# Sums of query-key products over head rows: from TensorE and PSUM to accumulating DMAs, with a new order of the GLU and down blocks

## The chip, the cores and the metric

The kernel runs on one core of one Trainium2 chip. The metric is the device time of one execution in microseconds (us). The core's engines are named as in the profile: PE (TensorE, matrix products into PSUM), DVE (VectorE, elementwise), ACT (ScalarE, here mostly copies out of PSUM), POOL (GpSimd) and SP (SyncE, here the queue that issues nearly all DMAs). Each engine runs its own instructions in order, and engines wait for one another only through semaphores. "SPq" is work of SP's queue; "PEld" is the loading of weights into TensorE, which overlaps its matmuls.

## The reference, cut to what matters

```python
x = A_x                                   # [1, 2048, 640]
xn = layernorm(x)
# A: attention with 32 heads of 20; each position looks at 8 positions, 2 apart, at and before it
qkv = xn @ wqkv                           # wqkv [640, 1920]
logits = sum_d(q * k_gathered) * 20**-0.5 # masked where the position would be below 0
attn = softmax(logits over the 8)
a = sum_w(attn * v_gathered) @ wo         # wo [640, 640]
# B: gated linear unit without a nonlinearity
b = ((xn @ w_gate) * (xn @ w_up)) @ w_down   # 640 -> 1536 -> 640
out = x + a + b
```

Everything is bf16 at the inputs and the output.

## The kernel before, in words

The feature dimension lies on the 128 partitions in five chunks of 128 (`NCH = 5`); time lies along the free dimension. The columns of `wqkv` are taken with stride five (`wcols`, L413), so that one head's 20 features fall on four neighbouring partitions in each of the five chunks: head 0 on partitions 0 to 3, head 31 on 124 to 127. A logit is then a sum over five chunks and four partitions.

**Stages.** First come the layer norm and the transposes to `XNT` (until about 32 us). Then PE runs one long list of work, the "fill": the rest of the Q and K projections (`proj`, L420, 20 items of five matmuls at L424), the V projections (20 items), and then blocks of the GLU and of the output. A GLU block `add_gu(j)` (L719) covers 512 positions with 24 items (12 gate, 12 up, five matmuls each, L577 in `glu`); ACT copies gate into `HT` and up into the ring `USX`, and DVE multiplies them ("h", L582). An output block `add_dn(j)` (L724) covers the same 512 positions with four tiles of 128 rows, each in two halves of 320 columns (`tail`, L592): 12 matmuls with `WD` over `HT` and 5 with `WO` over the attention output in `VO` (L608). DVE then adds the residual `XR` to PSUM and writes `FOUT` ("fin", L612), and SP stores it.

**Attention on DVE.** The sequence is cut in two halves h of 1024 positions. For each half there are four pairs p of window offsets (`pair`, L778; `qk_steps`, L458): DVE multiplies Q with shifted K for three chunks into `SL` (6144 elements a partition) and for two chunks into `TMP` (4096), and adds two of the chunks (L475, 4096), so that three are left. PE then sums the three chunks and the four partitions of each head in one step: `qk_logits` (L478) multiplies with the 0/1 matrix `G`, 12 matmuls a pair, into PSUM banks 6 and 7, which the rest of the fill therefore does not use; ACT scales them into `LOG` (L492), and POOL masks the first positions (L496). `softmax_steps` (L499) is split into a head (three max steps and a subtraction on DVE, the exponential on ACT) and a rest (sums, reciprocal, product). `attn_move` (L530) spreads the result over the head's four partitions in 16 DMAs a half. `pv_steps` (L536) forms the weighted sum of V for 256 positions; there are eight (pv 0 to 7), pv 0 to 3 with the first half's weights. Tile t of the output needs pv number t // 2.

**Order.** One Python program emits all engines' instructions. It keeps two clocks of its own, `t_pe` and `t_dve`, with a booked cost for each step; after each DVE step (`step`, L771) `run_fill` (L747) emits fill items until PE's clock has caught up. This fixes the order on each engine: which copy comes before which exponential on ACT, which h comes before which attention step on DVE. It fixes no times; on the chip an engine waits only for its data and for buffers to come free. The class `Sched` works out the semaphores from the bytes that each instruction reads and writes. Before, the fill's blocks are in the order gu 0, gu 1, dn 0, gu 2, dn 1, gu 3, dn 2, dn 3. `WD` and `WO` share their memory with `SL`, and their loads (`down_loads`, `out_loads`) are put on SP's queue after the last logits.

Of the kernel before, what the change touches and what calls it, by code (L numbers as in the profile page):

```python
# [26 lines left out]
NEG = -1e9  # L27
# [185 lines left out]
def build_kernel(nc, A_x, A_wqkv, A_wo, B_x, B_w_gate, B_w_up, B_w_down, out):  # L213
# [50 lines left out]
    NXR = 3  # L264
    XR = sb("XR", [128, NXR, D])
    FOUT = sb("FOUT", [128, 2, D])
    NUS = 6
# [9 lines left out]
    G = sb("G", [128, H], FP16)  # L277
# [4 lines left out]
    def dma(o, i, r=(), w=(), name="", eng="sp", group=None):  # L282
# [43 lines left out]
    def late_loads():  # L326
        wqkv_load(2)
# [92 lines left out]
    def proj(which, m, j):  # L420
# [9 lines left out]
        op("act", lambda e: e.activation(o, PS[:, b, :], ACT.Copy), r=[PS[:, b, :]], w=[o], name=f"pev{which}_{m}_{j}")  # L430
# [16 lines left out]
    def part_evac(which, t0, nt, m0, nm, b, col):  # L447
# [3 lines left out]
        op("act", lambda e: e.activation(o, i, ACT.Copy), r=[PS[:, b, :]], w=[o], name=f"ppev{which}_{m0}_{t0}")  # L451
# [326 lines left out]
    def pair(h, p):  # L778
# [3 lines left out]
        for it in qk_steps(h, p, s):  # L782
            step(it)
# [84 lines left out]
```

## Time and profile before

| what | value |
|---|---|
| time, median of 3 runs | 262.41 us (262.13 to 262.52) |
| the profiled execution's own time | 262.42 us |
| its span, first to last instruction | 260.7 us |
| TensorE clock granted | 1.000 |
| busy: PE, DVE, ACT, POOL | 255.6, 216.1, 107.3, 6.7 us |
| DMA, mean over the span | 23.46 MB, 90 GB/s |

The profile has several views. The page gives each engine's busy time and, in 40 equal slices of the span (6.5 us each), its busy share in tenths. The chain of waits goes back from the last instruction, at each step to whatever released it. The groups by line give the busy time, the count and the mean duration of one instruction. The timeline gives single instructions with start and duration. A duration holds some overlap with the next instruction of the same engine, so the spacing of two starts in an unbroken run is a better price for one more instruction than its duration.

### The profile page before, as it was taken

Reading aid. Unit: us, or ns where it says so; the run is one execution under the profiler, and the core shown is the slowest. Engines: PE = TensorE matmul, PEld = TensorE weight load, DVE = VectorE, ACT = ScalarE, POOL = GpSimd, SP = SyncE. Lnnn points to the kernel's source line nnn. Section 1 sums busy time; section 2 is a strip of 40 time slices with the busy share of each in tenths; the row PEclk is TensorE's granted clock in tenths of the full one; section 3 lists DMA queues with packets and bytes.
Section 4 is the critical chain, followed back from the end, with each engine's and each line's share of the span. In section 5 each row is a group of like instructions: output and inputs, shape, how many; then the busy total and the mean of one; then the engine's idle time right before and its main releaser. Section 6 shows DMA issues by size and latency. Waiting matters only on the chain.

```text
span 260.7 us, 4018 instructions
## 1 busy us (share of the span) xinstructions
PE 255.6 (98%) x1669; PEld 150.7 (58%) x1669; DVE 216.1 (83%) x240; ACT 107.3 (41%) x193; POOL 6.7 (3%) x13
## 2 busy tenths in 40 slices
PE   7999999899999999999999999999999999999996
PEld 3899855354554444444467744446774444777775
DVE  5799889999999999998847999999999999422221
ACT  3565558555657555565630035551004555000000
POOL 2000050000200000000000000000000000000000
DMA  6968889400000275065001376000311000021301
GB/s 202 326 136 148 100 226 402 156 3 0 0 3 0 50 206 144 0 208 219 3 0 57 97 199 175 0 4 0 99 54 50 0 3 0 27 74 53 101 28 50
DMA packets 21922, 23.46 MB, mean 90 GB/s; under 512 B 9872, under 2 KB 19472, under 8 KB 21904
## 3 DMA queue, kind: packets, MB, share of 16 engines
q1 hardware_dynamic: 21760, 23.04, 31.2%
q8 instruction: 13, 0.21, 0.3%
q10 hardware_dynamic: 144, 0.16, 0.2%
q14 instruction: 5, 0.04, 0.0%
HBM read 14.42 MB, written 2.62 MB: 65 GB/s over the span
## 4 chain that ended last, share of the span: by engine, by line
PE 80%; DVE 14%; SPq 2%; DMA 2%; ACT 1%; issue 1%
PE PS L577 40%; PE PS L608 28%; PE PS L424 10%; DVE SL L467 3%; SPq L283 2%; DVE XNS L371 2%; PE PS L485 2%; DVE STATS L354 2%; DVE SL L475 2%; DVE TMP L467 2%; DVE STATS L348 2%; DMA XST<-in_A_x_dram 2%; DVE MV L360 1%; DVE SD L369 1%; ACT KH L451 0%
## 5 line engine op out<-in xcount | busy, mean ns | idle before, releaser
L577 PE MATMUL PS<-XNT,WG 128*128 128x512 bf16 x240 | 59.6, 379 | 0.0
L577 PE MATMUL PS<-XNT,WU 128*128 128x512 bf16 x240 | 59.6, 379 | 0.0
L608 PE MATMUL PS<-WD,HT 128*128 128x320 bf16 (+1 forms) x396 | 57.6, 295 | 0.0
L579 ACT ACTIVATE HT<-PS 128x512 bf16<-128x512 f32 x48 | 28.7, 598 | 58.2 <-PE PS L577 58.2
L608 PEld LDWEIGHTS PS<-WD,HT 128*128 128x128 bf16 x396 | 38.1, 98 | 14.7
L551 DVE TENSOR_TENSOR PVB<-VO,ATB 128x10240 f16<-128x10240 bf16 x8 | 43.9, 5488 | 0.1
L424 PE MATMUL PS<-XNT,WQKV 128*128 128x512 bf16 x200 | 43.9, 379 | 0.0
L612 DVE TENSOR_TENSOR FOUT<-PS,XR 128x320 bf16<-128x320 f32 (+1 forms) x33 | 15.5, 477 | 30.4 <-PE PS L608 30.1
L577 PEld LDWEIGHTS PS<-XNT,WU 128*128 128x128 bf16 x240 | 23.4, 98 | 28.5 <-issue 0.4
L577 PEld LDWEIGHTS PS<-XNT,WG 128*128 128x128 bf16 x240 | 23.4, 98 | 28.2 <-issue 0.4
L579 ACT ACTIVATE USX<-PS 128x512 bf16<-128x512 f32 x48 | 28.7, 597 | 22.2 <-PE PS L577 20.8
L424 PEld LDWEIGHTS PS<-XNT,WQKV 128*128 128x128 bf16 x200 | 23.3, 118 | 20.2 <-issue 0.8
L546 DVE TENSOR_TENSOR PVB<-PVB 128x5120 f16<-128x5120 f16 (+1 forms) x16 | 34.4, 2150 | 0.0
L467 DVE TENSOR_TENSOR SL<-QH,KH 128x6144 f16<-128x6144 bf16 x8 | 26.8, 3352 | 1.4 <-ACT KH L451 1.4
L608 PE MATMUL PS<-WO,VO 128*128 128x320 bf16 (+1 forms) x165 | 27.1, 295 | 0.0
L582 DVE TENSOR_TENSOR HT<-HT,USX 128x512 bf16<-128x512 bf16 x48 | 18.5, 417 | 4.2 <-ACT USX L579 4.2
L608 PEld LDWEIGHTS PS<-WO,VO 128*128 128x128 bf16 x165 | 15.9, 98 | 5.9
L475 DVE TENSOR_TENSOR SL<-SL,TMP 128x4096 f16<-128x4096 f16 x8 | 18.3, 2290 | 0.2
L467 DVE TENSOR_TENSOR TMP<-QH,KH 128x4096 f16<-128x4096 bf16 x8 | 18.4, 2302 | 0.0
L430 ACT ACTIVATE VO<-PS 128x512 bf16<-128x512 f32 x20 | 11.9, 597 | 9.8 <-PE PS L424 9.8
L437 PE MATMUL PS<-XNT,WQKV 128*128 128x128 bf16 x200 | 12.6, 220 | 0.2
L437 PEld LDWEIGHTS PS<-XNT,WQKV 128*128 128x128 bf16 x200 | 11.6, 118 | 1.2 <-DVE XNT L394 0.5
(49 smaller groups left out, 137.8 us busy)
## 6 DMA issues: line engine op xcount, KB each, us to landing
ATB<-LOG SPq DMA_DIRECT2D x32, 128.0 KB, 2.6
XR<-in_A_x_dram SPq DMA_DIRECT2D x16, 160.0 KB, 2.3
XST<-in_A_x_dram SPq DMA_DIRECT2D x15, 160.0 KB, 3.9
out_dram<-FOUT SPq DMA_DIRECT2D x15, 160.0 KB, 1.8
WG<-in_B_w_gate_dram SPq DMA_DIRECT2D x1, 1920.0 KB, 9.5
WU<-in_B_w_up_dram SPq DMA_DIRECT2D x1, 1920.0 KB, 13.8
WD<-in_B_w_down_dram SPq DMA_DIRECT2D x1, 1920.0 KB, 8.2
WQKV<-in_A_wqkv_dram SPq DMA_DIRECT2D x10, 160.0 KB, 3.8
```

The lines of the kernel that those rows point to most:

```text
L424: op("pe", (lambda l, x, c: lambda e: e.matmul(PS[:, b, :], l, x, start=(c == 0), stop=(c == NCH - 1)))(l, x, c), r=[l, x], w=[PS[:, b, :] ...
L430: op("act", lambda e: e.activation(o, PS[:, b, :], ACT.Copy), r=[PS[:, b, :]], w=[o], name=f"pev{which}_{m}_{j}")
L437: op("pe", (lambda o, l, x, st, sp: lambda e: e.matmul(o, l, x, start=st, stop=sp))(o, l, x, st, sp), r=[l, x], w=[o], name=f"pp{which}_{m ...
L467: return lambda: op("dve", lambda e: e.tensor_tensor(o[:], qw, kw, ALU.mult), r=[q, k], w=[o[:]], name=f"prod{h}_{p}_{c0}")
L475: lambda: op("dve", lambda e: e.tensor_tensor(a, a, b, ALU.add), r=[a, b], w=[a], name=f"psum{h}_{p}")),
L546: return lambda: op("dve", lambda e: e.tensor_tensor(o, x, y, ALU.add), r=[x, y], w=[o], name=f"{name}_{b}")
L551: lambda: op("dve", lambda e: e.tensor_tensor(PVB[:], vw, aw, ALU.mult), r=[v, a], w=[PVB[:]], name=f"pv_{b}")),
L577: op("pe", (lambda l, x, c: lambda e: e.matmul(PS[:, b, :], l, x, start=(c == 0), stop=(c == NCH - 1)))(l, x, c), r=[l, x], w=[PS[:, b, :] ...
L579: op("act", lambda e: e.activation(o, PS[:, b, :], ACT.Copy), r=[PS[:, b, :]], w=[o], name=f"guev{which}_{m}_{j}")
L582: h_pending.append(lambda: op("dve", lambda e: e.tensor_tensor(h, h, o, ALU.mult), r=[h, o], w=[h], name=f"h{m}_{j}"))
L608: op("pe", (lambda l, x, i, b: lambda e: e.matmul(PS[:, b, 0:wid], l, x, start=(i == 0), stop=(i == n - 1)))(l, x, i, b), r=[l, x], w=[PS[ ...
L612: op("dve", (lambda o, xr, b: lambda e: e.tensor_tensor(o, PS[:, b, 0:wid], xr, ALU.add))(o, xr, b), r=[PS[:, b, :], xr], w=[o], name=f"fi ...
```

## The change

- **Logits.** The `G` matmuls, the ACT copies of their results and POOL's mask step go. For each pair, DVE forms the five chunk products one by one (2048 elements each: chunk 4 into a buffer `PE_`, chunks 0 and 1 into a slot `PP`, chunks 2 and 3 into `TMP`), adds `TMP` to the slot (4096) and the slot's halves (2048). A DMA issued by POOL adds the result to `PE_` ("acc", 512 KB). Then four DMAs gather the four partitions of each head: the first, issued by SP, copies 128 KB into `LOG`, the other three, issued by POOL, add to it ("row" 0 to 3). Each waits for the one before. `chain_stage` puts them on the queues: acc of pair n, then rows 2 and 3 of pair n-1, then rows 0 and 1 of pair n. There are two slots `PP` and five buffers `PE_`, some of them in the memory of `PVB`, `WD` and `WO`.
- **Scale and mask.** The scale moves into the Q copies on ACT. The mask becomes one small DVE addition of a prepared tile.
- **`attn_move`** issues 4 DMAs of 512 KB a half in place of 16 of 128 KB; `LOG`, `ATB` and the maxima become fp16.
- **Residual.** Rows 0 to 1535 of x are copied to the output by one DMA from DRAM to DRAM (`xinit`). For tiles 0 to 11 ACT, not DVE, copies PSUM into `FACC`, and a DMA issued by POOL adds it to the output rows ("oacc"). Tiles 12 to 15 stay as before.
- **Order.** The fill becomes gu 0, gu 1, gu 2, dn 0, gu 3, dn 1, dn 2, dn 3. Block 2's `HT` takes the place of the part of `XNT` that is no longer read, and of `LOG`. All eight PSUM banks serve the fill, `USX` has 7 slots for 6, and pairs (1,0) and (1,1) both go ahead of the first softmax; pv 0 and pv 1 go ahead of the second.

```diff
-    NKC = 3
-    NSL = 3
-    WD = sb("WD", [128, NF, D], at=a_pr)
-    WO = sb("WO", [128, NCH, D], at=a_pr + NF * D * 2)
-    SL = [sb(f"SL{s}", [128, 2, NKC, HS], FP16) for s in range(NSL)]
-    PVB = sb("PVB", [128, NCH, W, SB], FP16, at=place[0] - 2 * NKC * HS * 2)
-    TMP = sb("TMP", [128, 2, NCH - NKC, HS], FP16)
+    WD = sb("WD", [128, NF, D])
+    WO = sb("WO", [128, NCH, D])
+    PSB = [128, NSB, 2, SB]
+    PP = [sb(f"PP{s}", [128, 2] + PSB[1:], FP16, at=a_pr + 2 * s * HS * 4) for s in range(2)]
+    PE_ = [sb("PE0", PSB, FP16, at=a_pr + 4 * HS * 4)]
+    a_pv = place[0]
+    PVB = sb("PVB", [128, NCH, W, SB], FP16)
+    TMP = sb("TMP", [128, 2] + PSB[1:], FP16, at=a_pv)
+    for s in range(3):
+        PE_.append(sb(f"PE{s + 1}", PSB, FP16, at=a_pv + (2 + s) * HS * 4))
...
-        ATB.append(sb(f"ATB{h}", [128, NSB, W, SB], at=place[0]))
+        ATB.append(sb(f"ATB{h}", [128, NSB, W, SB], FP16, at=place[0]))
+        if h == 0:
+            PE_.append(sb("PE4", PSB, FP16, at=place[0] + NSB * W * SB * 2))
...
-    LOG = [sb(f"LOG{h}", [128, W, SB]) for h in range(2)]
-    M1 = sb("M1", [128, 4, SB])
-    M2 = sb("M2", [128, 2, SB])
-    M3 = sb("M3", [128, SB])
+    LOG = [sb(f"LOG{h}", [128, W, SB], FP16) for h in range(2)]
+    HX = sb("HX", [128, NF - 2 * NCH, JB], at=a_log)
...
-    NXR = 3
+    NXR = 2
+    TLAST = 12
     XR = sb("XR", [128, NXR, D])
-    FOUT = sb("FOUT", [128, 2, D])
-    NUS = 6
+    NFO = 3
+    FOUT = sb("FOUT", [128, NFO, D])
+    FACC = sb("FACC", [128, NFO, D], FP16, at=place[0] - NFO * D * 2)
+    NUS = 7
...
+    op("pool", lambda e: e.memset(MASK[:], 0.0), w=[MASK[:]], name="mask0")
+    op("pool", lambda e: e.memset(MSK0[:], 0.0), w=[MSK0[:]], name="msk0")
+    op("pool", lambda e: e.affine_select(MSK0[:], MSK0[:], pattern=[[DIL, W], [1, PAD]], compare_op=ALU.is_ge, fill=NEG,
+                                         base=-PAD, channel_multiplier=0), r=[MSK0[:]], w=[MSK0[:]], name="msk1")
...
     def late_loads():
+        dma(MASK[0:128:4], MSK0[0:32], r=[MSK0[0:32]], w=[MASK[0:128:4]], name="mask")
         wqkv_load(2)
...
+        sc = SCALE if which == 0 else 1.0
+        op("act", lambda e: e.activation(o, PS[:, b, :], ACT.Copy, scale=sc), r=[PS[:, b, :]], w=[o],
+           name=f"pev{which}_{m}_{j}")
...
-    def qk_steps(h, p, s):
-        kept, tmp = SL[s], TMP
-        kp = KH[h][:, 0, 0:1].ap[0]
-        def prod(o, c0, c1):
-            q = QH[h][:, c0:c1, :]
-            k = KH[h][:, c0:c1, 4 * p:4 * p + HS + 2]
-            kw = bass.AP(k.tensor, k.offset, [kp, [2, 2], [KL, c1 - c0], [1, HS]])
-            qw = q.unsqueeze(1).to_broadcast([128, 2, c1 - c0, HS])
-            return lambda: op("dve", lambda e: e.tensor_tensor(o[:], qw, kw, ALU.mult), r=[q, k], w=[o[:]],
-                              name=f"prod{h}_{p}_{c0}")
-        a, b = kept[:, :, 0:NCH - NKC, :], tmp[:]
+    def qk_steps(h, p, s, en):
+        slot, first = PP[s], PE_[en]
+        def prod(o, c):
+            q = QH[h][:, c, :]
+            k = KH[h][:, c, 4 * p:4 * p + HS + DIL]
+            qw = bass.AP(q.tensor, q.offset, [q.ap[0], [SB, NSB], [0, 2], [1, SB]])
+            kw = bass.AP(k.tensor, k.offset, [k.ap[0], [SB, NSB], [DIL, 2], [1, SB]])
+            return (1.22, lambda: op("dve", lambda e: e.tensor_tensor(o, qw, kw, ALU.mult), r=[q, k], w=[o],
+                                     name=f"prod{h}_{p}_{c}"))
+        a, b = slot[:], TMP[:]
+        return [prod(first[:], 4), prod(slot[:, 0], 0), prod(slot[:, 1], 1), prod(TMP[:, 0], 2), prod(TMP[:, 1], 3)] + [
+            (2.3, lambda: op("dve", lambda e: e.tensor_tensor(a, a, b, ALU.add), r=[a, b], w=[a], name=f"psum{h}_{p}")),
+            (1.22, lambda: op("dve", lambda e: e.tensor_tensor(a[:, 0], a[:, 0], a[:, 1], ALU.add), r=[a], w=[a[:, 0]],
+                              name=f"psun{h}_{p}")),
+        ]
+    def acc(o, i, name):
+        op("pool", lambda e: e.dma_start(o, i, accum_op=ALU.add), r=[o, i], w=[o], dma=True, name=name)
+    def qk_chain(h, p, s, en):
+        slot, first = PP[s], PE_[en]
+        dst = LOG[h][:, 2 * p:2 * p + 2, :]
+        def row(r):
+            x = first[r:128:4]
+            return bass.AP(x.tensor, x.offset, [x.ap[0], [2 * SB, NSB], [1, 2 * SB]])
         return [
-            (0.16 + 2 * NKC * HS / 1920, prod(kept, 0, NKC)),
-            (0.16 + 2 * (NCH - NKC) * HS / 1920, prod(tmp, NKC, NCH)),
-            (0.16 + 2 * (NCH - NKC) * HS / 1920,
-             lambda: op("dve", lambda e: e.tensor_tensor(a, a, b, ALU.add), r=[a, b], w=[a], name=f"psum{h}_{p}")),
+            lambda: acc(first[:], slot[:, 0], f"acc{h}_{p}_0"),
+            lambda: dma(dst, row(0), r=[first[:]], w=[dst], name=f"row{h}_{p}_0"),
+            lambda: acc(dst, row(1), f"row{h}_{p}_1"),
+            lambda: acc(dst, row(2), f"row{h}_{p}_2"),
+            lambda: acc(dst, row(3), f"row{h}_{p}_3"),
         ]
-    def qk_logits(h, batch):
-        for p, s in batch:
-            lb = 6 + p % 2
-            for c in range(NKC):
-                for q in range(NSB):
-                    o = PS[32 * q:32 * q + 32, lb, :]
-                    x = SL[s][:, :, c, q * SB:(q + 1) * SB]
-                    op("pe", (lambda o, x, q, c: lambda e: e.matmul(o, G[:], x, start=(c == 0), stop=(c == NKC - 1),
-                                                                 tile_position=(0, 32 * q)))(o, x, q, c),
-                       r=[G[:], x], w=[o], name=f"lg{h}_{p}_{c}_{q}")
-        for p, s in batch:
-            lb = 6 + p % 2
-            o = LOG[h][:, 2 * p:2 * p + 2, :]
-            i = PS[:, lb, :].rearrange("p (w s) -> p w s", w=2)
-            op("act", (lambda o, i: lambda e: e.activation(o, i, ACT.Copy, scale=SCALE))(o, i),
-               r=[PS[:, lb, :]], w=[o], name=f"lgev{h}_{p}")
-        if h == 0 and batch[-1][0] == 3:
-            m = LOG[0][0:32, :, 0:PAD]
-            op("pool", lambda e: e.affine_select(m, m, pattern=[[DIL, W], [1, PAD]], compare_op=ALU.is_ge, fill=NEG,
-                                                 base=-PAD, channel_multiplier=0), r=[m], w=[m], name="mask")
...
-        head = [
+        first = LOG[h][:, :, 0:PAD]
+        head = [(0.25, tt(first, first, MASK[:], ALU.add, "mask"))] if h == 0 else []
+        head += [
...
     def attn_move(h):
-        for r in range(4):
-            for q in range(NSB):
-                src, dst = LOG[h][32 * q:32 * q + 32], ATB[h][r:128:4, q]
-                dma(dst, src, r=[src], w=[dst], name=f"atb{h}_{q}_{r}", group=("atb", h))
+        for q in range(NSB):
+            x, dst = LOG[h][q:128:4], ATB[h][:, q]
+            src = bass.AP(x.tensor, x.offset, [x.ap[0], [0, 4], [1, W * SB]])
+            dma(dst, src, r=[x], w=[dst], name=f"atb{h}_{q}")
...
+    def ht(j, m):
+        if j != 2:
+            return HT[:, j % 3 % 2, m, :]
+        if m < 2 * NCH:
+            return XNT[:, m % NCH, m // NCH * JB:(m // NCH + 1) * JB]
+        return HX[:, m - 2 * NCH, :]
...
-                    l, x = HT[:, j % 2, i, rows], WD[:, i, cols]
+                    l, x = ht(j, i)[:, rows], WD[:, i, cols]
...
-            o = FOUT[:, t % 2, cols]
+            if t < TLAST:
+                o = FACC[:, t % NFO, cols]
+                op("act", (lambda o, b: lambda e: e.activation(o, PS[:, b, 0:wid], ACT.Copy))(o, b),
+                   r=[PS[:, b, :]], w=[o], name=f"fin{t}_{nb}")
+                continue
+            o = FOUT[:, t % NFO, cols]
             xr = XR[:, t % NXR, cols]
             op("dve", (lambda o, xr, b: lambda e: e.tensor_tensor(o, PS[:, b, 0:wid], xr, ALU.add))(o, xr, b),
                r=[PS[:, b, :], xr], w=[o], name=f"fin{t}_{nb}")
             if last:
                 stores.append(dma(ohbm[t * TS:(t + 1) * TS, cols], o, r=[o], name=f"odma{t}_{c0}"))
-        if nb == 1 and not last:
-            f = FOUT[:, t % 2, :]
+        if nb == 1 and t < TLAST:
+            f, d = FACC[:, t % NFO, :], ohbm[t * TS:(t + 1) * TS, :]
+            stores.append(op("pool", lambda e: e.dma_start(d, f, accum_op=ALU.add), r=[f, ("out",)], w=[("out", t)],
+                             dma=True, name=f"oacc{t}"))
+        elif nb == 1 and not last:
+            f = FOUT[:, t % NFO, :]
             stores.append(dma(ohbm[t * TS:(t + 1) * TS, :], f, r=[f], name=f"odma{t}"))
             if t + NXR < NT:
                 xr_load(t + NXR)
...
-    bank_ring[:] = [b for b in bank_ring if b < 6]
...
-    t_pe, t_dve = [31.0], [31.8]
+    t_pe, t_dve = [31.0], [33.2]
...
     add_gu(0)
     add_gu(1)
+    add_gu(2)
     add_dn(0)
-    add_gu(2)
+    add_gu(3)
     add_dn(1)
-    add_gu(3)
     add_dn(2)
     add_dn(3)
...
-    def take():
-        h, batch, at = batches.pop(0)
-        qk_logits(h, batch)
-        t_pe[0] = max(t_pe[0], at) + 0.44 + 0.2175 * NKC * len(batch)
-        if h == 1 and batch[-1][0] == 3:
-            down_loads()
-            out_loads()
-            loaded.append(True)
-    def run_fill(until, upto=None):
...
-                t_dve[0] += 0.48
+                t_dve[0] += 0.48 if it[1] * 2 >= TLAST else 0.0
...
+    ring = []
+    def chain_stage(new):
+        new[0]()
+        if ring:
+            ring[-1][0]()
+            ring[-1][1]()
+        new[1]()
+        new[2]()
+        ring.append(new[3:])
...
-        for it in qk_steps(h, p, s):
+        n = 4 * h + p
+        en = (1, 2, 3, 0, 1, 2, 0, 4)[n]
+        for it in qk_steps(h, p, n % 2, en):
             step(it)
-        return p, s
-    def batch(h, pairs):
-        batches.append((h, pairs, t_dve[0] + 0.3))
-    def settle():
-        while batches:
-            run_fill(batches[0][2] + 0.01)
-        t_dve[0] = max(t_dve[0], t_pe[0] + 1.6)
-    batch(0, [pair(0, 0), pair(0, 1)])
-    batch(0, [pair(0, 2), pair(0, 3)])
+        chain_stage(qk_chain(h, p, n % 2, en))
+    def drain():
+        ring[-1][0]()
+        ring[-1][1]()
+    def settle(lag):
+        t_dve[0] = max(t_dve[0], lag)
...
+    for p in range(4):
+        pair(0, p)
+    a_end = t_dve[0]
     headA, restA = softmax_steps(0)
     force_fill(QKB)
     t_dve[0] = max(t_dve[0], t_pe[0] + 0.8)
-    b0 = pair(1, 0)
-    settle()
+    pair(1, 0)
+    pair(1, 1)
+    settle(a_end + 18.0)
+    flush_h(1)
     for it in headA:
         step(it)
-    batch(1, [b0, pair(1, 1)])
+    t_dve[0] += 1.6
     for it in restA:
         step(it)
     attn_move(0)
-    batch(1, [pair(1, 2), pair(1, 3)])
-    for t in range(NXR):
+    pair(1, 2)
+    pair(1, 3)
+    b_end = t_dve[0]
+    drain()
+    down_loads()
+    out_loads()
+    loaded.append(True)
+    dma(ohbm[0:TLAST * TS, :], xhbm[0:TLAST * TS, :], w=[("out",)], name="xinit")
+    for t in range(TLAST, TLAST + NXR):
         xr_load(t)
     force_fill(VB)
...
     headB, restB = softmax_steps(1)
     pv(0)
-    settle()
+    pv(1)
+    settle(b_end + 18.0)
+    flush_h(1)
     for it in headB:
         step(it)
-    bank_ring[:] = bank_ring + [6, 7]
-    pv(1)
+    t_dve[0] += 1.6
     for it in restB:
         step(it)
     attn_move(1)
```

More of the change, by code (lines that the diff above doesn't have):

```diff
@@ L26 @@
 EPS = 1e-5
-NEG = -1e9
+NEG = -30000.0
 VP = 32
@@ L450, in part_evac @@
         i = PS[:, b, col:col + nm * nt * TS].rearrange("p (m s) -> p m s", m=nm)
-        op("act", lambda e: e.activation(o, i, ACT.Copy), r=[PS[:, b, :]], w=[o], name=f"ppev{which}_{m0}_{t0}")
+        sc = SCALE if which == 0 else 1.0
+        op("act", lambda e: e.activation(o, i, ACT.Copy, scale=sc), r=[PS[:, b, :]], w=[o], name=f"ppev{which}_{m0}_{t0}")
     def k_seam():
@@ L571, in glu @@
         T = (WG, WU)[which]
-        h = HT[:, j % 2, m, :]
+        h = ht(j, m)
         o = (h, USX[:, k, :])[which]
@@ L730, in build_kernel, with run_fill @@
     add_gu(1)
+    add_gu(2)
     add_dn(0)
-    add_gu(2)
+    add_gu(3)
     add_dn(1)
-    add_gu(3)
     add_dn(2)
     add_dn(3)
-    def take():
-        h, batch, at = batches.pop(0)
-        qk_logits(h, batch)
-        t_pe[0] = max(t_pe[0], at) + 0.44 + 0.2175 * NKC * len(batch)
-        if h == 1 and batch[-1][0] == 3:
-            down_loads()
-            out_loads()
-            loaded.append(True)
-    def run_fill(until, upto=None):
+    def run_fill(until):
         while t_pe[0] < until and pos[0] < len(fill):
-            if batches and t_pe[0] >= batches[0][2]:
-                take()
-                continue
             it = fill[pos[0]]
@@ L763, in run_fill @@
             pos[0] += 1
-        while batches and (t_pe[0] >= batches[0][2] or until >= batches[0][2]):
-            take()
     def force_fill(n):
```

19 lines of the change are left out of this document (5 added, 14 removed).

## The prediction

> **What bounds the kernel now.** I read the page first: busy times and the 40 slices.
>
> ```profile
> span 260.7 us, 4018 instructions
> ...
> PE 255.6 (98%) x1669; PEld 150.7 (58%) x1669; DVE 216.1 (83%) x240; ACT 107.3 (41%) x193; POOL 6.7 (3%) x13
> ...
> PE   7999999899999999999999999999999999999996
> ...
> DVE  5799889999999999998847999999999999422221
> ACT  3565558555657555565630035551004555000000
> ```
>
> PE is busy in every slice after the first. DVE is nearly full until slice 34 and then mostly idle. Busy PE alone proves little, so I read the chain of waits in order of time.
>
> ```profile
> 49.35 0.83 PE PS L485 x12
> 50.18 14.16 PE PS L424 x65
> 64.34 1.44 PE PS L485 x24
> ...
> 86.41 1.41 PE PS L485 x24
> ...
> 110.59 1.41 PE PS L485 x24
> ...
> 132.61 18.47 PE PS L608 x136
> 151.08 25.90 PE PS L577 x120
> ...
> 221.35 37.00 PE PS L608 x289
> 258.38 0.33 DVE FOUT L612
> ```
>
> From 49 us to the end the chain never leaves PE: one matmul follows another, whatever DVE and the DMAs do. The logits (L485) are links of that chain. So PE's work sets the end, and a microsecond taken from PE is a microsecond of the kernel as long as nothing else becomes late.
>
> **What PE loses.** The last three logit batches cost 1.44 + 1.41 + 1.41 = 4.26 us. The first two stand in the timeline of PE:
>
> ```profile
> 30.03 17.65 PE L424 MATMUL PS<-XNT,WQKV 128*128 128x512 bf16 x80
> ...
> 50.11 14.22 PE L424 MATMUL PS<-XNT,WQKV 128*128 128x512 bf16 x65
> ```
>
> A matmul of 512 columns takes 25.90 / 120 = 0.216 us in an unbroken run, so 80 of them need 17.3 us and the next could start at 47.3, not 50.11: 2.8 us, of them 0.9 waiting. Sum 7.1. A check over the whole: (200 + 480) x 0.216 + 18.47 x 2 + 37.00 = 220.7, from 30.03 to 250.7, while the chain has PE's end at 258.4: 7.6. I take 7.4 us, between the two. The change adds no matmul. Reordering gu and dn blocks leaves their number as it is.
>
> With nothing else late the times on PE are, from 30.0: V done 73.2, gu 0 99.1, gu 1 125.0, gu 2 150.9, dn 0 169.4, gu 3 195.3, dn 1 213.8, the rest 250.8. What follows the last matmul (L612, one store) is unchanged. The profiled execution took 262.42, 1.7 more than its span, and the median of the runs is 262.41, so one basis serves: 262.4 - 7.4 = **255.0**.
>
> **DVE's new price.** Rows of the timeline of DVE, then groups by line:
>
> ```profile
> 33.56 3.36 DVE L467 TENSOR_TENSOR SL<-QH,KH 128x6144 f16<-128x6144 bf16 x1 [1.36 <-ACT KH L451]
> ...
> 39.20 2.29 DVE L475 TENSOR_TENSOR SL<-SL,TMP 128x4096 f16<-128x4096 f16 x1
> 41.41 3.35 DVE L467 TENSOR_TENSOR SL<-QH,KH 128x6144 f16<-128x6144 bf16 x1
> ...
> 64.81 3.35 DVE L467 TENSOR_TENSOR SL<-QH,KH 128x6144 f16<-128x6144 bf16 x1
> ...
> 72.69 0.69 DVE L501 TENSOR_TENSOR M<-LOG 128x1024 bf16<-128x1024 bf16 x1
> ...
> 74.20 1.23 DVE L516 TENSOR_TENSOR LOG<-LOG,M 128x2048 bf16<-128x2048 bf16 x1
> 75.34 3.35 DVE L467 TENSOR_TENSOR SL<-QH,KH 128x6144 f16<-128x6144 bf16 x1
> ...
> 83.47 0.68 DVE L501 TENSOR_TENSOR S<-LOG 128x1024 f16<-128x1024 bf16 x1
> ...
> 88.19 3.35 DVE L467 TENSOR_TENSOR SL<-QH,KH 128x6144 f16<-128x6144 bf16 x1
> ...
> 160.25 5.49 DVE L551 TENSOR_TENSOR PVB<-VO,ATB 128x10240 f16<-128x10240 bf16 x1
> ...
> 169.40 0.75 DVE L582 TENSOR_TENSOR HT<-HT,USX 128x512 bf16<-128x512 bf16 x2
> ...
> 172.66 5.49 DVE L551 TENSOR_TENSOR PVB<-VO,ATB 128x10240 f16<-128x10240 bf16 x1
> ```
> ```profile
> L579 ACT ACTIVATE HT<-PS 128x512 bf16<-128x512 f32 x48 | 28.7, 598 | 58.2 <-PE PS L577 58.2
> L612 DVE TENSOR_TENSOR FOUT<-PS,XR 128x320 bf16<-128x320 f32 (+1 forms) x33 | 15.5, 477 | 30.4 <-PE PS L608 30.1
> ```
>
> By spacing of starts, 2048 elements take 75.34 - 74.20 = 1.14 us and 4096 take 41.41 - 39.20 = 2.21. A pair before took 41.41 - 33.56 = 7.85; after, five products and one half sum of 1.14 and one sum of 2.21 make 9.05. Eight pairs: +9.6 us. The 24 residual sums that leave DVE give back 24 x 0.48 = 11.4. They cost ACT at most 24 x 0.60 = 14 us, in stretches where its slices show 0, and each tile half occupies a bank for 2.3 us, so ACT hides them. DVE's total stays about level; its order decides.
>
> **DVE's times after.** Pairs 0 to 3 run from 33.6 to 69.8. Two more pairs (18.1) and some eight h of 0.35 (half of 0.75, rounded down for overlap) bring DVE to 90.7, the first softmax. Its head takes 75.34 - 72.69 = 2.65 plus 0.2 for the mask, the exponential is waited for (2.4), the rest takes 88.19 - 83.47 = 4.7 with one h: 100.7. Pairs 6 and 7 with nine h: 122. One pv with six h takes 172.66 - 160.25 = 12.4, 10.4 without; pv 0 ends at 134.4, pv 1 at 146.8, the second softmax at 157.5, pv 2 and 3 at 168 and 178, and pv 4 to 7 (with gu 3's twelve h) at about 190, 202, 213, 224. PE wants them at 150.9, 160.1, 195.3, 204.5, 213.8, 223.0, 232.3, 241.5. The smallest slack is 13 us, at pv 1. So DVE is no bound unless the logits come late.
>
> **The DMAs that replace the matmuls.** No accumulating DMA and no DMA from POOL is in this trace. The nearest rows, of DMA issues and of the timelines of POOL and ACT:
>
> ```profile
> ATB<-LOG SPq DMA_DIRECT2D x32, 128.0 KB, 2.6
> ...
> WD<-in_B_w_down_dram SPq DMA_DIRECT2D x1, 1920.0 KB, 8.2
> ...
> WO<-in_A_wo_dram SPq DMA_DIRECT2D x1, 800.0 KB, 9.7
> ```
> ```profile
> 33.59 3.43 POOL L455 COPY KH<-KH 128x70 bf16<-128x70 bf16 x1 [31.09 <-ACT KH L451]
> 66.57 1.77 POOL L496 TENSOR_SCALAR_AFFINE_SELECT LOG<-LOG 32x112 bf16<-32x112 bf16 x1 [29.55 <-ACT LOG L492]
> ```
> ```profile
> 78.31 1.90 ACT L518 ACTIVATE LOG<-LOG 128x2048 bf16<-128x2048 bf16 x1
> ```
>
> A 128 KB move inside SBUF lands after 2.6 us. The WD load moves 1920 / 8.2 = 234 KB a us, so 384 KB more add 1.6: a plain 512 KB move lands after 4.2. Adding reads the target too, so as upper bounds I double both: acc 4.2 to 8.4, a row 2.6 to 5.2. I take 5.5 and 3.2, nearer the plain moves, as much of a small move is latency. A POOL issue I put at 1.0 (0 to 1.8, the shorter of POOL's two rows).
>
> POOL's queue holds acc(n), rows 2 and 3 of pair n-1, row 1 of pair n; row 0 is on SP. The loop is: acc issued and landed, row 0 issued (0.6) and landed, row 1 issued, next acc. Period 5.5 + 0.6 + 2.6 + 1.0 = 9.7 us; bounds 7.4 (then DVE's 9.05 rules) and 8.4 + 0.6 + 2.6 + 1.8, plus as much again for the second issue = 15.2. With period T, acc(4) is issued at 42.6 + 4T; row 1 of pair 3, just ahead of it, then needs 2.2 more, and rows 2 and 3 follow with 3.2 each, and a hop: the first half's logits land at about 51.6 + 4T. At 9.7 that is 90.4, against DVE's 90.7: just in time. The slots `PP` ask that acc(2) has landed by 71, and at 9.7 it lands at 67.5.
>
> **How late may they be?** The exponential is an ACT instruction, and all later copies out of PSUM are queued behind it. By its own booked costs the program's clock for DVE stands at 33.2 + 4 x 9.62 = 71.7 after four pairs, at 92.5 after six with four h, and at 95.4 after the head; it puts the exponential behind the copies of fill items up to that time, which PE reaches about 94.5. From there eight banks of 1.08 us (five matmuls) keep PE going until 103. Logits, head, 1.90 for the exponential and 0.60 for one copy must be done by then: logits by about 97.6, T up to 11.5. Past that each us of lateness is a us of PE.
>
> For the second half six issues drain after pair 7 (122): about 20 us, so 142, against 146.8 when DVE asks; there 13 us more could be absorbed.
>
> **Loads that move.** WD and WO now wait for acc(7) and for row 3 of pair 6, about 130, and on SP stand behind row 0 of pair 7; with 8.2 and 9.7 us they land by 141, wanted at 150.9: 10 us of cover. `xinit` and the XR loads are queued behind them, and dn 0's oacc wait for it; three `FACC` slots of 4.6 us and eight banks hide that. `attn_move` has 8 issues for 32: SP is freer. The mask DMA delays the V and GLU weights by one issue, 0.6 us, and PE wants those at 51.6 and 73.
>
> **A rule against the change.** In both POOL rows the instruction ends with the DVE product that runs beside it: 33.59 + 3.43 = 37.02 against 33.56 + 3.36 = 36.92, and 66.57 + 1.77 = 68.34 against 64.81 + 3.35 = 68.16. POOL was held by DVE. If POOL's DMA issues are held in the same way, acc waits out a product (1.14) and row 1 half of one (0.6): T = 11.5, on the edge, 255 to 258 us. The Trainium skill, SBUF — State Buffer (Who interferes with whom), says that a DVE instruction with two SBUF inputs contends with a GpSimd instruction that reads SBUF, not with one that only writes it; by that the two rows are explained and writing descriptors would go free, 255. The same page's Summary: rules for kernel authors says without that exception not to hide a GpSimd DMA under DVE in its fast modes. This trace has no POOL DMA to tell.
>
> **The rivals.**
> 1. *The chain is late and ACT carries it to PE* (slower). For it: POOL rows held by DVE, four issues a pair in series, no cover beyond 7 us. Against: the plain moves are short. Place: the first exponential. Loss = 51.6 + 4T - 97.6; at T = 13.3 it eats the 7.4 us, above that the kernel is slower; at the bound 15.2 the loss is 15 us, and 21 with rows at their bound too: 270 to 276 us. The Trainium skill, DMA: Bandwidth & Descriptors (Anatomy of one DMA — SWDGE (gpsimd) path), gives 2.0 us plus bytes at 436 GB/s for a plain GpSimd DMA; by that estimate acc would be 3.2 and T 7.4.
> 2. *Half late*: T between 11.5 and 13, or POOL held: 255.5 to 261.5 us.
> 3. *WD, WO or a pv late*: the drain takes 10 us longer than I say, by issues held under pv products of 5.49 us. PE then stands before dn 0: 256 to 260 us.
> 4. *The removal does not shorten PE*, since other waits open up in its place (T near 13.3): about 262. Little speaks for just this balance.
>
> **How the numbers follow.** The clean case 0.61 (255.1 us, range of its own 254.4 to 256.5); rival 2 0.11, rival 3 0.06; rival 4 0.05; rival 1 0.17. A measurement of this kernel tells 0.2%, 0.5 us, from no change. Faster 0.61 + 0.11 + 0.06 = 0.78, same 0.05, slower 0.17. The range reaches from the clean case's low end to the end of rival 2, 261.5, and leaves out rivals 4 and 1 but for a little.
>
> **What would show it right or wrong.** Right: no L485 group; the PE blocks start at the times above within 1 us; a chain that stays on PE; spacing of pairs on DVE near 9 us; the first max of the softmax not waiting long for a DMA; ACT's exponential starting by 100. Wrong: PE idle behind ACT near 103, acc landing after more than 8 us, pairs spaced wider than 11 us, PE idle before the first L608 block with WD or WO as releaser, or POOL issues that end with DVE instructions. The forecast falls if T is above 13.

## The result, and the profile after

| kernel | median, us | lowest to highest | runs |
|---|---|---|---|
| before | 262.35 | 262.13 to 262.52 | 4 |
| after | 255.91 | 255.46 to 257.01 | 4 |

The ratio is 0.9761 (95% interval 0.9729 to 0.9793): 6.4 us faster, where 7.3 were forecast (255.1). The profiled execution of the changed kernel took 255.46 with a span of 253.2. Its page, busy times and the slices of PE:

```profile
PE 249.0 (98%) x1573; PEld 149.0 (59%) x1573; DVE 217.8 (86%) x249; ACT 113.7 (45%) x209; POOL 41.0 (16%) x56
...
PE   7999999999999999999999999999999999999996
```

PE is as full as before and has 96 matmuls less (1573 for 1669); DVE's total has moved by 1.7 us only. The chain of waits after, its end in order of time:

```profile
30.10 43.17 PE PS L432 x200
73.26 77.70 PE PS L593 x360
150.96 18.47 PE PS L624 x136
169.44 25.90 PE PS L593 x120
195.34 55.48 PE PS L624 x425
250.84 0.32 DVE FOUT L633
```

From 30 us on one matmul follows another, with no other engine between, and no group of logit matmuls (L485 of the kernel before) is left. The forecast starts were 73.2, 150.9, 169.4, 195.3 and 250.8; each came within 0.1 us. PE's end moved from 258.38 to 250.84, that is 7.5 us against the 7.4 of the sum.

The timeline of DVE after (a wait and its releaser stand in brackets): products of pairs 0, 4 and 6, a sum, steps of both softmaxes, and the ends of pv 1 and pv 2.

```profile
33.42 1.23 DVE L477 TENSOR_TENSOR PE<-QH,KH 128x2048 f16<-128x2048 bf16 x1 [1.35 <-ACT KH L462]
...
70.52 1.22 DVE L477 TENSOR_TENSOR PE<-QH,KH 128x2048 f16<-128x2048 bf16 x1
...
76.32 2.29 DVE L482 TENSOR_TENSOR PP<-PP,TMP 128x4096 f16<-128x4096 f16 x1
...
91.61 0.21 DVE L508 TENSOR_TENSOR LOG<-LOG,MASK 128x112 f16<-128x112 f16 x1
...
99.47 0.69 DVE L508 TENSOR_TENSOR S<-LOG 128x1024 f16<-128x1024 f16 x1 [4.89 <-ACT LOG L527]
...
104.74 1.22 DVE L477 TENSOR_TENSOR PE<-QH,KH 128x2048 f16<-128x2048 bf16 x1
...
150.21 0.82 DVE L555 TENSOR_TENSOR VO<-PVB 128x1280 bf16<-128x1280 f16 x1
...
154.31 0.69 DVE L508 TENSOR_TENSOR M<-LOG 128x1024 f16<-128x1024 f16 x1 [2.25 <-DMA LOG<-PE]
...
173.50 0.82 DVE L555 TENSOR_TENSOR VO<-PVB 128x1280 bf16<-128x1280 f16 x1
```

A pair takes (70.52 - 33.42) / 4 = 9.27 us, forecast 9.05. The first softmax starts at 91.6 with no wait for the logits (forecast 90.7). The second waits 2.25 us for them, a wait that costs nothing: pv 2 ends at 174.3, and PE wants it at 195.3.

The timelines of POOL, SP's queue and ACT, and the groups of DMA issues (KB each, median us from issue to landing):

```profile
33.45 1.30 POOL L466 COPY KH<-KH 128x70 bf16<-128x70 bf16 x1 [30.97 <-ACT KH L462]
43.13 1.00 POOL L488 DMA_DIRECT2D PE<-PP  x1 [8.39 <-DVE PP L483]
54.16 0.88 POOL L488 DMA_DIRECT2D LOG<-PE  x1 [10.02 <-DMA LOG<-PE]
54.70 1.21 POOL L488 DMA_DIRECT2D PE<-PP  x1
...
63.38 1.21 POOL L488 DMA_DIRECT2D PE<-PP  x1
...
71.22 1.21 POOL L488 DMA_DIRECT2D PE<-PP  x1
...
77.41 0.86 POOL L488 DMA_DIRECT2D LOG<-PE  x1 [2.87 <-DMA LOG<-PE]
...
80.16 0.84 POOL L488 DMA_DIRECT2D PE<-PP  x1 [0.78 <-DVE PP L483]
...
87.19 1.76 POOL L488 DMA_DIRECT2D LOG<-PE  x2 [4.86 <-DMA LOG<-PE]
...
96.56 0.86 POOL L488 DMA_DIRECT2D LOG<-PE  x1 [3.84 <-DMA LOG<-PE]
...
141.11 0.86 POOL L488 DMA_DIRECT2D LOG<-PE  x1 [6.68 <-DMA LOG<-PE]
```
```profile
51.78 0.60 SPq L293 DMA_DIRECT2D LOG<-PE  x1
```
```profile
97.54 1.90 ACT L527 ACTIVATE LOG<-LOG 128x2048 f16<-128x2048 f16 x1
```
```profile
PE<-PP POOLq DMA_DIRECT2D x8, 512.0 KB, 4.8
...
LOG<-PE POOLq DMA_DIRECT2D x24, 128.0 KB, 2.8
...
WD<-in_B_w_down_dram SPq DMA_DIRECT2D x1, 1920.0 KB, 10.2
...
WO<-in_A_wo_dram SPq DMA_DIRECT2D x1, 800.0 KB, 5.6
```

At the median the accumulating DMAs are short: 4.8 us for 512 KB (taken at 5.5) and 2.8 for 128 KB (taken at 3.2). The first acc is not: SP issues the row that waits for it only at 51.78, 8.6 us after the acc's own issue at 43.13. The load of `WU` (issued at 35.61, 16.1 us) runs beside it until 51.7. The accs start 11.6, 8.7 and 7.8 us apart; the fifth, at 80.16, waits for DVE and no longer for the chain. By the order on POOL's queue (acc of pair 4, rows 2 and 3 of pair 3, row 1 of pair 4) the last row of the first half is the first of the two at 87.19: about 87.2 + 2.8 = 90.0, forecast 90.4.

### The profile page after: what moved, and what is told of

Its sections match the earlier page's. It is cut to its first block, busy times and chain, and to the rows that moved or that the text cites. A ratio compares the mean times of both kernels' runs of the same rounds, so it can differ in the third digit from the quotient of the medians.

```text
span 253.2 us, 3849 instructions
## 1 busy us (share of the span) xinstructions
PE 249.0 (98%) x1573; PEld 149.0 (59%) x1573; DVE 217.8 (86%) x249; ACT 113.7 (45%) x209; POOL 41.0 (16%) x56
## 3 DMA queue, kind: packets, MB, share of 16 engines
q0 software_dynamic: 6336, 9.31, 23.7%
## 4 chain that ended last, share of the span: by engine, by line
PE 97%; DVE 1%; DMA 1%; ACT 0%; issue 0%
PE PS L593 41%; PE PS L624 29%; PE PS L432 17%; PE PS L447 5%; PE PS L454 4%; DMA XST<-in_A_x_dram 1%; PE PS L393 1%; DVE STATS L356 0%; ACT XNT L404 0%; DVE XNS L379 0%; PE PS L410 0%; DVE STATS L362 0%; DVE FOUT L633 0%; DVE MV L368 0%; DVE SD L377 0%
## 5 line engine op out<-in xcount | busy, mean ns | idle before, releaser
L624 PE MATMUL PS<-WD,HT 128*128 128x320 bf16 (+1 forms) x300 | 43.2, 294 | 0.0
L624 PEld LDWEIGHTS PS<-WD,HT 128*128 128x128 bf16 x300 | 28.7, 98 | 10.9
L432 PEld LDWEIGHTS PS<-XNT,WQKV 128*128 128x128 bf16 x200 | 23.5, 117 | 19.5
L488 POOL DMA_DIRECT2D LOG<-PE x24 | 21.9, 925 | 58.5 <-DMA LOG<-PE 58.5
L628 ACT ACTIVATE FACC<-PS 128x320 f16<-128x320 f32 x24 | 10.5, 436 | 41.8 <-PE PS L624 41.8
L639 POOL DMA_DIRECT2D out_dram<-FACC x12 | 10.2, 851 | 71.2 <-ACT FACC L628 71.2
L477 DVE TENSOR_TENSOR TMP<-QH,KH 128x2048 f16<-128x2048 bf16 x16 | 19.1, 1218 | 0.0
L477 DVE TENSOR_TENSOR PP<-QH,KH 128x2048 f16<-128x2048 bf16 x16 | 19.0, 1221 | 0.0
L482 DVE TENSOR_TENSOR PP<-PP,TMP 128x4096 f16<-128x4096 f16 x8 | 18.3, 2291 | 0.2
L633 DVE TENSOR_TENSOR FOUT<-PS,XR 128x320 bf16<-128x320 f32 (+1 forms) x9 | 4.1, 454 | 15.6 <-PE PS L624 15.6
## 6 DMA issues: line engine op xcount, KB each, us to landing
WU<-in_B_w_up_dram SPq DMA_DIRECT2D x1, 1920.0 KB, 16.1
WD<-in_B_w_down_dram SPq DMA_DIRECT2D x1, 1920.0 KB, 10.2
```

What stands on the lines that cost most here:

```text
L432: op("pe", (lambda l, x, c: lambda e: e.matmul(PS[:, b, :], l, x, start=(c == 0), stop=(c == NCH - 1)))(l, x, c), r=[l, x], w=[PS[:, b, :] ...
L477: return (1.22, lambda: op("dve", lambda e: e.tensor_tensor(o, qw, kw, ALU.mult), r=[q, k], w=[o], name=f"prod{h}_{p}_{c}"))
L482: (2.3, lambda: op("dve", lambda e: e.tensor_tensor(a, a, b, ALU.add), r=[a, b], w=[a], name=f"psum{h}_{p}")),
L488: op("pool", lambda e: e.dma_start(o, i, accum_op=ALU.add), r=[o, i], w=[o], dma=True, name=name)
L624: op("pe", (lambda l, x, i, b: lambda e: e.matmul(PS[:, b, 0:wid], l, x, start=(i == 0), stop=(i == n - 1)))(l, x, i, b), r=[l, x], w=[PS[ ...
L628: op("act", (lambda o, b: lambda e: e.activation(o, PS[:, b, 0:wid], ACT.Copy))(o, b), r=[PS[:, b, :]], w=[o], name=f"fin{t}_{nb}")
```

## The experiments

The theory: PE's 96 matmuls are the whole gain, and the rest of the change is what keeps PE fed without them. The rivals: the new order of blocks is the gain; or waits that opened elsewhere took part of it.

**1. The matmuls back.** In the changed kernel four groups of 24 matmuls, shaped as the logit matmuls were, go into gu 0, with a result that nothing reads.

```diff
+            if j == 0 and m in (1, 4, 7, 10):
+                fill.append((1.41, idle_logits))
```

> The changed kernel with four groups of 24 extra matmuls put into GLU block 0, of the shape of the removed logit matmuls (32 output rows, 512 columns); nothing reads their results, so the output is unaffected. Theory (the end is set by PE's list of work, so PE time counts in full): a batch of 24 cost 1.41 us in the chain of before, so 4 x 1.41 = 5.6 us more than the changed kernel, about 261.5 us. Rival (after the change DVE or the DMAs set the end, and PE has room): within 1 us of the changed kernel, 255.5 to 257.

Measured: 261.66, ratio to before 0.9981 (0.9966 to 0.9996). One group in PE's timeline:

```profile
76.63 1.48 PE L747 MATMUL PS<-XNT,IDENT 128*32 128x512 bf16 x24
78.04 1.25 PE L593 MATMUL PS<-XNT,WG 128*128 128x512 bf16 x5
```

By the spacing 1.41 us a group, 5.6 in all; the kernel lost 5.8. PE's time counts in full. That the change gained more, 7.5 us on PE, fits the prediction's reading of before, where the first two batches cost 2.8 us with a wait between them, and not 1.4.

**2. Before without the logit matmuls.** ACT takes the logits from the product sums, so the sums over chunks and partitions are left out.

```diff
-                    op("pe", ... matmul(o, G[:], x, ...
-            i = PS[:, lb, :].rearrange("p (w s) -> p w s", w=2)
+            i = SL[s][:, :, 0, 0:SB]
...
-        t_pe[0] = max(t_pe[0], at) + 0.44 + 0.2175 * NKC * len(batch)
+        t_pe[0] = max(t_pe[0], at)
```

> The kernel before with only the logit matmuls left out; ACT copies part of the product sums into the logits instead, so the logits are not the reference's. No accumulating DMA, old order of the blocks. Theory: the 7.1 us that the logits took from PE come off, less about 1 us, since dn 0 then wants pv 1 at 136.4 and DVE has it at about 137.6: 255.3 to 257.5 us. Rival (the gain needs the new order too, or comes from it): above 259 us.

Measured: 264.56, ratio 1.0099 (1.0082 to 1.0116). A miss: slower than before, with less work. The timelines of PE and DVE of this kernel:

```profile
143.25 1.51 PE L599 MATMUL PS<-WO,VO 128*128 128x320 bf16 x5 [7.12 <-DVE VO L537]
```
```profile
121.62 0.42 DVE L573 TENSOR_TENSOR HT<-HT,USX 128x512 bf16<-128x512 bf16 x1 [1.46 <-ACT USX L570]
123.78 0.42 DVE L573 TENSOR_TENSOR HT<-HT,USX 128x512 bf16<-128x512 bf16 x1 [1.74 <-ACT USX L570]
125.94 0.42 DVE L573 TENSOR_TENSOR HT<-HT,USX 128x512 bf16<-128x512 bf16 x1 [1.73 <-ACT USX L570]
127.62 0.49 DVE L603 TENSOR_TENSOR FOUT<-PS,XR 128x320 bf16<-128x320 f32 x1 [1.26 <-PE PS L599]
...
129.93 0.49 DVE L603 TENSOR_TENSOR FOUT<-PS,XR 128x320 bf16<-128x320 f32 x1 [1.49 <-PE PS L599]
...
131.80 5.48 DVE L542 TENSOR_TENSOR PVB<-VO,ATB 128x10240 f16<-128x10240 bf16 x1
```

PE waits 7.12 us for pv 1, and by the chain of waits the 56 matmuls after it take 9.34 us, where the same number in the 18.47 us of 136 takes 7.6: together 8.8 us. DVE had lost 1.46 + 1.74 + 1.73 + 1.26 + 1.49 = 7.7 us ahead of it, in the second softmax, on h and residual steps whose input PE had not made yet. My edit took the matmuls' cost out of the program's own clock too; so its plan, which fixes DVE's order, put these steps too early. The edit changed two things, and number 3 parts them.

**3. The same with the plan kept.** As number 2, and the sums are left out in the same way, but the line that books the cost of the matmuls stays.

```diff
         t_pe[0] = max(t_pe[0], at) + 0.44 + 0.2175 * NKC * len(batch)
```

> As the run of the kernel before without its logit matmuls (the logits again are not the reference's), but the program's own clock still books the matmuls' cost, so that DVE keeps the residual sums of dn 0 where they stood. In the earlier run DVE waited 7.7 us between the max steps of the second softmax, behind h and residual steps that PE had not yet fed, and PE then waited 7.1 us for pv 1. Theory (the loss was that placement, not DVE's load): pv 1 ends near 136, wanted at 136.0, and the time is 255 to 258 us. Rival (in the old order DVE cannot bring pv 1 in time, however it is placed): PE waits 5 us or more before the third tile of dn 0, and the time is above 260 us.

Measured: 255.17, ratio 0.9734 (0.9720 to 0.9748). One booked line is worth 9.4 us here: in the profiles the spans are 262.2 and 253.4 us, the 8.8 us of number 2 apart, and PE has no wait for pv 1. With the old order of blocks, the removal of the matmuls alone gives what the change gives, though this kernel leaves the sums out and so is no replacement for it.

**4. Before with the new order alone.**

```diff
     add_gu(0)
     add_gu(1)
+    add_gu(2)
     add_dn(0)
-    add_gu(2)
+    add_gu(3)
     add_dn(1)
-    add_gu(3)
```

> The kernel before with the new order of the blocks alone (three GLU blocks ahead of dn 0, block 2's products in the unused part of XNT and LOG as in the change); the logits stay matmuls. Theory: PE has the same work and no wait to lose, so 262.0 to 262.8 us, no change. Rival (the order by itself brings part of the gain): 260 us or less.

Measured: 262.36, ratio 1.0008 (0.9994 to 1.0022). The order by itself gains nothing.

**5. After with the old order.** The diff of number 4 the other way.

> The changed kernel with the blocks in the old order (gu 0, gu 1, dn 0, gu 2, dn 1, gu 3, dn 2, dn 3) and the HT buffers as before. Theory: the DMA sums bring the attention and the WD and WO loads later than the matmul sums did, and the third GLU block ahead is what covers that. dn 0 would stand ready at 125.0, WD lands about 142 and WO about 145, pv 0 ends about 137: PE stands still some 17 to 19 us, 272 to 276 us. Rival (the order matters little): within 2 us of the changed kernel.

Measured: 278.86, ratio 1.0627 (1.0571 to 1.0683). The wait came as expected; the time came about 3 us above the forecast range. PE's timeline, and one stretch of the view by windows (behind POOL's busy time stand the granted clock, that is the share of TensorE's full speed, the DMA share and GB/s):

```profile
142.75 3.38 PE L620 MATMUL PS<-WD,HT 128*128 128x320 bf16 x12 [17.19 <-DMA WD<-in_B_w_down_dram]
...
203.12 1.51 PE L620 MATMUL PS<-WO,VO 128*128 128x320 bf16 x5 [2.24 <-DVE VO L555]
```
```profile
142.70:150.00 7.30, 7.25 (x34) 4.39 (x35) 6.32 (x4) 0.44 (x1) 0.10 (x1) 0.62 1.01 367
```

`WD` cannot be loaded before the chain of DMAs has left its memory, and with the old order PE wants it at 125. After the wait of 17.19 us the granted clock was 0.62 for 7 us; the block of 136 matmuls took 21.34 us in the chain for 18.47, 2.9 us more. A second wait, 2.24 us at 203.12, is for a pv: DVE had stood 17.8 us ahead of the second softmax, behind an h that PE's own stop delayed. The 56 matmuls after it took 9.32 us for 7.6, 1.7 more. The four make 24.0 us of the 24.5 by which the profiled execution's span (277.7) exceeds that of the changed kernel; the forecast had the first alone. So the order brings no time, but it is what the DMA chain costs in cover: without it the change loses 16.5 us to before.

**6. A longer chain.** One chunk sum per pair goes from DVE to a second accumulating DMA of 512 KB.

```diff
-            (1.22, lambda: op("dve", ... tensor_tensor(a[:, 0], a[:, 0], a[:, 1], ALU.add) ...
+            (1.22, lambda: None),
...
             lambda: acc(first[:], slot[:, 0], f"acc{h}_{p}_0"),
+            lambda: acc(first[:], slot[:, 1], f"acc{h}_{p}_1"),
...
```

On POOL's queue the second acc of a pair stands between rows 2 and 3 of the pair before.

> The changed kernel with one chunk sum moved from DVE to the DMAs: per pair two accumulating DMAs of 512 KB, one after the other, and no half sum on DVE; the order on PE and ACT is the same. Theory (rival 1 of the prediction is real but lies beyond this kernel): the loop's period goes from about 8.3 to 13.2 us, the first half's logits land at about 109 instead of 91, 11 us past the 97.6 that ACT's exponential allows, and PE waits: about 267 us, 262 to 272. Rival (the DMA chain has ample cover): within 1 us of the changed kernel.

Measured: 265.57, ratio 1.0155 (1.0095 to 1.0215). The chain of waits of this kernel, and the timeline of PE:

```profile
59.41 4.95 DMA PE<-PP
...
72.08 4.98 DMA PE<-PP
...
84.70 4.98 DMA PE<-PP
...
103.62 4.34 DMA LOG<-PE
108.23 0.70 DVE M L508
...
111.01 1.91 ACT LOG L527
...
113.46 47.59 PE PS L593 x210
```
```profile
113.46 2.31 PE L593 MATMUL PS<-XNT,WG 128*128 128x512 bf16 x5 [7.89 <-ACT HT L595]
115.56 2.32 PE L593 MATMUL PS<-XNT,WU 128*128 128x512 bf16 x5
```

This is the prediction's first rival made real: period 12.6 to 12.7, late logits, a late exponential, the copies behind it, PE idle for 7.89 us. Then two groups of five matmuls take 2.1 us by spacing where 1.08 is usual, 2 us more. PE stopped at 113.46 - 7.89 = 105.6, where I had put 103. From the logits to PE's restart it took 113.46 - 108.2 = 5.3 us, so logits at 100.3 would still have been in time; those of the changed kernel came at about 90.0, so its slack is some 10 us. By the prediction's 51.6 + 4T the gain would stand on T staying below (100.3 - 51.6) / 4 = 12.2. That is an estimate that no run measures: here, with T at 12.65, the formula gives 102.2, and the logits landed at 103.62 + 4.34 = 108.0, since row 3 stands behind the next pair's second acc.

**7. The residual back on DVE.** In the changed kernel, DVE adds all residuals, SP stores all tiles; run twice, in two sessions.

```diff
-    TLAST = 12
+    TLAST = 0
-    dma(ohbm[0:TLAST * TS, :], xhbm[0:TLAST * TS, :], w=[("out",)], name="xinit")
```

> The changed kernel with the residual as before for all tiles: no copy of x to the output, no accumulating store, DVE adds the residual of all 16 tiles. Theory: 24 more DVE steps of 0.41 us move pv 7 from 231.5 to about 241.5, and PE wants it at 243.1, so nothing is lost: within 0.7 us of the changed kernel. Rival (DVE's relief is part of the gain): 257.5 us or more.

> The changed kernel with the residual on DVE, a second time, as the candidate for the best version. So far 255.4 us, with 1.82 us outside its span where the changed kernel has 2.28 and the kernel before 1.72. Theory (the accumulating stores cost some 0.45 us outside the span and save nothing on PE): 255.2 to 255.6 us, 1.8 outside the span. Rival (the difference was chance): 255.6 us or more, or 2.2 outside the span.

Measured: 255.37, ratio 0.9731 (0.9718 to 0.9745), and 255.11, ratio 0.9725 (0.9712 to 0.9738). DVE can carry the residual (226.3 us busy); the part of the change that moved it gains nothing.

**8. After again.** The changed kernel as it is, beside the first run of number 7.

> The changed kernel again, unchanged, for the spread of its runs: the four runs so far had spans of 253.2 to 254.7 us where those of before lie within 0.4 us. Theory: PE's blocks stand where they stood, and the difference is a wait at the start (loads) or between gu 2 and dn 0; this profile shows which. Expected 255.4 to 257.0 us.

Measured: 255.82, ratio 0.9764 (0.9737 to 0.9790). It spends 2.27 to 2.33 us outside its span, number 7 spends 1.78 to 1.84, and before 1.66 to 1.80. Three runs look for that half microsecond.

**9. Plain stores by POOL.** The stores of tiles 0 to 11 don't add, so their residual is left out.

```diff
-            stores.append(op("pool", lambda e: e.dma_start(d, f, accum_op=ALU.add), r=[f, ("out",)], w=[("out", t)],
+            stores.append(op("pool", lambda e: e.dma_start(d, f), r=[f], w=[("out", t)],
...
-    dma(ohbm[0:TLAST * TS, :], xhbm[0:TLAST * TS, :], w=[("out",)], name="xinit")
```

> The changed kernel with the 12 stores still issued by POOL from FACC but without adding, and without the copy of x to the output; the residual of tiles 0 to 11 is left out. If adding in DRAM or the copy makes the 0.45 us outside the span: 1.8 outside, 255.2 to 255.6 us. If stores by POOL make it: 2.3 outside, 255.6 to 256.2 us.

Measured: 255.91, ratio 0.9757 (0.9744 to 0.9771); 2.12 to 2.19 outside the span, between the two answers. It looked as if POOL's stores were the cause. But number 6 has twelve adding stores and only 1.75 to 1.84. Among what differs there is how much POOL's queue carries, which the last two vary.

**10. Twelve POOL DMAs that store nothing,** added to number 7, **and 11. eight such DMAs** added to the changed kernel.

```diff
+                op("pool", lambda e: e.dma_start(g, f), r=[f], w=[g], dma=True, name=f"extra{t}")
```

> The kernel with the residual on DVE (runs outside its span 1.78 to 1.84 us), with twelve more DMAs issued by POOL, each moving one finished tile of FOUT to FACC inside SBUF, 160 KB; the output is unchanged. It has as many POOL packets as the changed kernel, but no store by POOL. If POOL's stores to DRAM cost the 0.45 us outside the span, it stays at 1.8 us there and at about 255.3 us in all. If what counts is the number of packets on POOL's queue (6336 in the kernels that show 2.1 to 2.4, against 4608 and 7488 in those that show 1.8), it shows 2.1 to 2.35 outside the span.

> The changed kernel (2.25 to 2.37 us outside its span), its twelve adding stores kept, with eight more POOL DMAs of 160 KB from FACC to FOUT inside SBUF, so that POOL's queue has 7488 packets, as in the kernel with two accumulating DMAs a pair, which showed 1.75 to 1.84. If the stores cost the 0.45 us, it stays at 2.25 to 2.4; if the number of packets decides, it falls to about 1.8. The span should stay within 0.5 us of 253.2 by either.

Measured: 255.60, ratio 0.9748 (0.9729 to 0.9768), with 2.10 to 2.18 outside the span; and 255.13, ratio 0.9724 (0.9701 to 0.9747), with 1.75 to 1.81. Outside the span, more work took less time. The line for POOL's queue (packets, MB, share), of after, of number 10 and of number 11:

```profile
q0 software_dynamic: 6336, 9.31, 23.7%
```
```profile
q0 software_dynamic: 6336, 9.31, 20.1%
```
```profile
q0 software_dynamic: 7488, 10.62, 25.7%
```

The stores are not what decides; the time goes with the amount on that queue, of which three values were tried: 6336 packets (44 DMAs) go with 2.1 to 2.4 us, with stores or without; 4608 (32) and 7488 (52) go with 1.75 to 1.84. Whether packets or DMAs are what counts, and why the middle value is the slow one, is open: the traces show nothing outside the span. Among kernels with 6336 the adding ones have some 0.15 us more.

## Why the prediction was right

None of the four rivals came about in the time. Two things that the prediction named as danger did occur, and cost nothing: the first acc landed after more than 8 us, and the last rows drained some 8 us more slowly than forecast, nearly the 10 us of rival 3. By the prediction's own steps:

**PE's work is the time.** Right, and shown in both directions: numbers 1 and 3 put the matmuls in and take them out, and each moves the time by their price. The 7.4 us taken between two workings came out as 7.5. That the order is neutral on PE, as the sum had it, is number 4.

**The DMA chain.** The bounds were 4.2 to 8.4 us for acc and 2.6 to 5.2 for a row; the medians of 4.8 and 2.8 lie near the plain moves, where the values were taken. The first acc, with 8.6 us beside the load of `WU`, lies above the upper bound; the prediction had no term for loads beside the chain. The period was 11.6 us at first and then 8.7 and 7.8, forecast 9.7. That the logits came within half a microsecond of the forecast is in part luck: one long period and two short ones nearly cancelled. By the formula of the Trainium skill, DMA: Bandwidth & Descriptors (Anatomy of one DMA — SWDGE (gpsimd) path), a plain 512 KB would take 3.2 us, an estimate; the measured 4.8 with adding lies above it, and the run shows no plain one from POOL to compare.

**POOL held by DVE.** POOL's copy of 70 columns of `KH` is held again: 33.45 + 1.30 = 34.75, the product beside it ends at 33.42 + 1.23 = 34.65. The issues are not: 0.86 us at 77.41, in the middle of the sum that DVE runs from 76.32 to 78.61, and 0.86 at 96.56, where DVE waits for the exponential. The Trainium skill, SBUF — State Buffer (Who interferes with whom), makes just this difference, and the trace agrees; the rule in the same page's Summary: rules for kernel authors, without the exception, would have the issues held too (T = 11.5 by the prediction's working), which the trace doesn't bear out. The one period of 11.6 us is the first acc's.

**DVE's times.** Late by more than forecast, at no cost. The exponential was waited for 4.89 us, not 2.4: ACT had it behind copies up to 97.04, by the plan's order. With some h more, the next pair began at 104.7, forecast 100.7, and pv 1 ended at 151.0, forecast 146.8. The smallest slack was 160.1 - 151.0 = 9 us instead of 13.

**The drain and the loads.** The second half's logits were forecast at 142 and were awaited until 154.3. Row 2 of the last pair is issued at 141.11 (POOL's timeline), beside the loads of weights and `xinit`, and lands 10.2 us later; the last row waits for it. That part of the forecast was 12 us off; some 4 of them are pair 7's later end on DVE (126.3, forecast 122). It was harmless only because the working had left 13, and because `WD` (131.73) and `WO` (139.56) were issued ahead of the last two rows (141.11 and 151.60). In SP's timeline `WD` and `WO` stand at:

```profile
131.73 0.59 SPq L293 DMA_DIRECT2D WD<-in_B_w_down_dram  x1
139.56 0.35 SPq L293 DMA_DIRECT2D WO<-in_A_wo_dram  x1
```

So `WO` landed at 139.56 + 5.6 = 145.2: 5.7 us of cover, not 10.

**The time outside the span.** This is the term that was mis-sized: "1.7 more than its span" was carried over, and it is 2.25 to 2.31. The sum forecast a span of 253.3, and the profiled one is 253.2; with 2.3 instead of 1.7 it gives 255.6. No run of before could have shown it, as no DMA of POOL is in that kernel. The rest to the median of 255.91 is a span that varies from 253.2 to 254.7 in this kernel. Every profile of it was taken at 253.2, so the cause of that spread stays open.

**The better version.** The residual on DVE with the rest of the change (255.11 and 255.37) and the changed kernel with eight further DMAs (255.13) are 0.5 to 0.8 us below the changed kernel. About 0.5 of it lies outside the span, in every run; in the whole time the intervals touch those of the changed kernel, so how much more there is stays open.

## What to carry to other kernels

Where one engine's instructions form the chain from early on to the end, take work from that engine and price it by its spacing; then list who becomes late next and by how much. When an order is fixed by a program's own clock, a removed step must keep or re-tune its booking, or the plan puts instructions where they wait: here 9.4 us. A reordering that gains nothing by itself can be the condition of another part, so test it both alone and left out.

## What the hardware showed unexpectedly

- The time outside the span depends on the amount that POOL's DMA queue has carried, and not in one direction: 1.75 to 1.84 us with 4608 or 7488 packets, 2.1 to 2.4 with 6336.
- A pause of PE costs more than itself, and not in proportion to its length: 1.7 us more after 2.2 us (number 5), 1.7 after 7.1 (number 2), 2 after 7.9 (number 6, where two groups ran at half speed), and 2.9 after 17.2 (number 5, granted clock 0.62 for 7 us).
- A small transfer beside large ones loses its price: 128 KB rows took 2.8 us at the median and up to 10.2 beside the loads of `WO` and x, and the first 512 KB acc took 8.6 beside that of `WU`, against a median of 4.8.
- Adding has its price: POOL's store of 160 KB to DRAM took 3.4 us at the median with adding (the changed kernel) and 2.1 without (number 9).
